# A fused convolution and channel-mix kernel: K in bundles of two slots, R's low channels as side-by-side tiles, and R and conv in two shared banks

## The chip, the cores and the metric

The kernel runs on one core of one Trainium2 chip. The metric is the device time of one execution in microseconds (us). Each kernel ran several times in rounds together with the kernel before on the same chip. Names in the trace: PE is TensorE, PEld its weight loads, DVE is VectorE, ACT is ScalarE, POOL is GpSimd, SP is SyncE.

## The reference, cut to what matters

```python
# x: (8, 4160, 192), weight: (8 heads, 7 taps)
w   = softmax(weight)
out = causal convolution of x over 7 positions, head h using w[h]     # "conv", gives y
x, x_prev = out, out shifted by one position
xk = mu_k * x + (1 - mu_k) * x_prev          # "mix"
xr = mu_r * x + (1 - mu_r) * x_prev
k  = maximum(xk @ w_k, 0)                    # 192 -> 1024      "K", "relu"
v  = k * k @ w_v                             # 1024 -> 192      "square", "V"
r  = sigmoid(xr @ w_r)                       # 192 -> 192       "R"
return r * v                                 # float32
```

The 192 channels are 128 "high" ones and 64 "low" ones. The kernel handles the batches in four pairs; for a pair, the low channels of the two batches fill partitions 0 to 63 and 64 to 127.

## The kernel before

The convolution is a product with a banded matrix, block by block of 112 positions (a "group" is several blocks). Its result y has positions on partitions. It is needed with channels on partitions, and gets there in one of two ways: by transposes on TensorE, for early groups, or by a write to DRAM and a transposing DMA read.

```python
two = ctx.enter_context(tc.tile_pool(name="two", bufs=2))
...
psK = ctx.enter_context(tc.tile_pool(name="psK", bufs=2, space=bass.MemoryType.PSUM))
psV = ctx.enter_context(tc.tile_pool(name="psV", bufs=2, space=bass.MemoryType.PSUM))
psM = ctx.enter_context(tc.tile_pool(name="psM", bufs=2, space=bass.MemoryType.PSUM))   # R, conv, transposes
...
def y_write(g):      # y -> DRAM
...
def y_read(g):       # DRAM -> yT, transposing
    nc.sync.dma_start_transpose(
        out=yTs[p][:, :, YC + r0 : YC + r1], in_=y_drams[p][r0:r1, :]
    )
...
def diff(s): ...     # d = yT[t] - yT[t-1]
def mix(s, i, part): # xk (i=0) or xr (i=1), high or low: d * mu + yT[t-1]
...
def r_mm(m):         # R of one row tile of 128
    ...
    nc.tensor.matmul(out=o, lhsT=hi, rhs=wr[:, 0, :], start=True, stop=False)
    nc.tensor.matmul(out=o, lhsT=lo, rhs=wlo, start=False, stop=True)   # 128 rows, half of wlo is zero
```

K's low channels already went as pairs of 64-row tiles that run side by side; R's did not. All work is placed by hand in tables of slots.

## Time and profile before

| kernel before | value | read from |
|---|---|---|
| time | 467.41 us (467.33 to 469.0) | 3 runs |
| span of the profiled run | 467.2 us | cores |
| TensorE, VectorE, ScalarE busy | 445.2, 390.4, 374.6 us | page, part 1 |
| TensorE's share of the chain that ended last | 91% | page, part 4 |
| clock granted to TensorE, mean | 0.990 | cores |

The prediction below shows these parts of the page and the timeline of a bundle. One more view: the waits, where each row reads "engine line waited for: us in total, times, longest us". These rows are what TensorE's convs (once the conv weights were there) and VectorE's difference waited for.

```profile
PE ps_c L199 <- DVE yT L268: 1.4, 4, 0.6
PE ps_c L199 <- ACT y L222: 0.9, 1, 0.9
DVE d L281 <- DMA yT<-y_dram: 0.2, 1, 0.2
```

### The profile page before, as it was taken

Reading aid. Unit: us, or ns where it says so; the run is one execution under the profiler, and the core shown is the slowest. Engines: PE = TensorE matmul, PEld = TensorE weight load, DVE = VectorE, ACT = ScalarE, POOL = GpSimd, SP = SyncE. Lnnn points to the kernel's source line nnn. Section 1 sums busy time; section 2 is a strip of 40 time slices with the busy share of each in tenths; the row PEclk is TensorE's granted clock in tenths of the full one; section 3 lists DMA queues with packets and bytes.
Section 4 is the critical chain, followed back from the end, with each engine's and each line's share of the span. In section 5 each row is a group of like instructions: output and inputs, shape, how many; then the busy total and the mean of one; then the engine's idle time right before and its main releaser. Section 6 shows DMA issues by size and latency. Waiting matters only on the chain.

```text
span 467.2 us, 9868 instructions
## 1 busy us (share of the span) xinstructions
PE 445.2 (95%) x3892; PEld 300.6 (64%) x3954; DVE 390.4 (84%) x616; ACT 374.6 (80%) x549; POOL 51.1 (11%) x71
## 2 busy tenths in 40 slices
PE   7788999999999999999999999999999999999996
PEld 3454766666776666666676666666676666666676
DVE  2778988797998879889798989978898987999873
ACT  2489888988879797888879788888978888777771
POOL 5812211000010041000002041000002000000000
PEclk9799999999999999999999999999999999999999
DMA  7996699972459599945367679937157753511222
GB/s 89 160 174 106 162 197 156 233 200 68 127 142 183 148 139 229 181 129 139 93 173 119 165 133 214 229 100 187 52 152 138 173 135 100 153 65 56 69 69 94
DMA packets 138942, 65.79 MB, mean 141 GB/s; under 512 B 89936, under 2 KB 138464, under 8 KB 138896
## 3 DMA queue, kind: packets, MB, share of 16 engines
q1 hardware_dynamic: 98000, 49.26, 41.0%
q0 software_dynamic: 40896, 15.90, 30.0%
q8 instruction: 31, 0.51, 0.4%
q14 instruction: 15, 0.12, 0.1%
HBM read 31.59 MB, written 37.52 MB: 148 GB/s over the span
## 4 chain that ended last, share of the span: by engine, by line
PE 91%; ACT 2%; issue 2%; DMA 2%; DVE 1%; DVEq 0%; ACTq 0%
PE ps_k L343 38%; PE ps_v L433 37%; PE ps_c L199 5%; PE ps_r L416 5%; PE ps_r L415 5%; ACT k_sb L372 1%; DMA w_scr<-w_row 1%; PE ps_k L360 1%; DMA toe<-w_scr 1%; ACT y L219 1%; DMA w_raw<-in_weight_dram 1%; PE ps_t L257 1%; DVE yT L268 0%; ACT y L222 0%; DVE k L391 0%
## 5 line engine op out<-in xcount | busy, mean ns | idle before, releaser
L372 ACT ACTIVATE k_sb<-ps_k 128x1024 bf16<-128x1024 f32 x260 | 260.2, 1026 | 35.8 <-PE ps_k L343 31.8
L343 PE MATMUL ps_k<-xk,wk 64*128 64x512 bf16 (+2 forms) x994 | 206.0, 376 | 9.5 <-ACT k_sb L372 0.9
L433 PE MATMUL ps_v<-wv,k 128*128 128x192 bf16 x2048 | 210.8, 246 | 0.0
L433 PEld LDWEIGHTS <-k 128*128 128x128 bf16 x2048 | 175.4, 98 | 30.6 <-issue 1.4
L391 DVE TENSOR_TENSOR k<-k_sb 128x1024 bf16<-128x1024 bf16 x256 | 174.8, 684 | 16.7 <-ACT k_sb L372 16.0
L343 PEld LDWEIGHTS <-wk 64*128 64x128 bf16 (+1 forms) x1056 | 56.2, 96 | 109.2 <-issue 107.9
L446 DVE TENSOR_TENSOR o_sb<-ps_v,r_sb 128x384 f32<-128x384 f32 x132 | 72.2, 547 | 39.6 <-PE ps_v L433 34.7
L423 ACT ACTIVATE r_sb<-ps_r 128x384 bf16<-128x384 f32 x132 | 64.3, 487 | 38.1 <-PE ps_r L416 37.3
L301 DVE SCALAR_TENSOR_TENSOR xr<-d,mu,yT 128x1024 bf16<-128x1024 bf16 (+1 forms) x66 | 65.1, 988 | 0.1
L301 DVE SCALAR_TENSOR_TENSOR xk<-d,mu,yT 128x1024 bf16<-128x1024 bf16 (+1 forms) x66 | 64.4, 977 | 0.2
L415 PE MATMUL ps_r<-wr,xr 128*128 128x192 bf16 x256 | 62.8, 246 | 0.0
L416 PE MATMUL ps_r<-wr,xr 128*128 128x192 bf16 x256 | 62.8, 246 | 0.0
L219 ACT CAST y<-ps_c 112x480 bf16<-112x480 f32 (+4 forms) x100 | 47.9, 483 | 10.4 <-PE ps_c L199 10.2
L199 PE MATMUL ps_c<-xb,toe 128*112 128x480 bf16 (+5 forms) x152 | 46.2, 332 | 5.3 <-DMA toe<-w_scr 2.9
L109 POOL DMA_DIRECT2D xb<-in_x_dram x38 | 34.9, 928 | 26.8 <-PE ps_c L199 15.9
L281 DVE TENSOR_TENSOR d<-yT 128x1536 bf16<-128x1536 bf16 (+2 forms) x37 | 31.8, 859 | 0.4 <-DMA yT<-y_dram 0.2
L108 POOL DMA_DIRECT2D xb<-in_x_dram x8 | 4.3, 538 | 215.7 <-PE ps_k L343 206.3
L199 PEld LDWEIGHTS <-toe 128*112 128x112 bf16 x152 | 19.2, 134 | 12.1 <-DMA toe<-w_scr 3.4
L222 ACT CAST y<-ps_c 112x480 bf16<-112x480 f32 (+8 forms) x53 | 25.2, 482 | 0.2 <-DVE yT L227 0.2
L415 PEld LDWEIGHTS <-xr 128*128 128x128 bf16 x256 | 25.0, 98 | 0.0
L416 PEld LDWEIGHTS <-xr 128*128 128x128 bf16 x256 | 25.0, 98 | 0.0
L103 POOL DMA_DIRECT2D xb<-in_x_dram x8 | 4.6, 581 | 62.4 <-PE ps_r L416 61.0
(46 smaller groups left out, 67.8 us busy)
## 6 DMA issues: line engine op xcount, KB each, us to landing
out_dram<-o_sb SPq DMA_DIRECT2D x128, 192.0 KB, 2.3
y_dram<-y SPq DMA_DIRECT2D x7, 840.0 KB, 5.0
xb<-in_x_dram POOLq DMA_DIRECT2D x12, 432.0 KB, 12.0
y_dram<-y SPq DMA_DIRECT2D x6, 756.0 KB, 4.6
xb<-in_x_dram POOLq DMA_DIRECT2D x8, 480.0 KB, 13.2
xb<-in_x_dram POOLq DMA_DIRECT2D x6, 384.0 KB, 6.6
y_dram<-y SPq DMA_DIRECT2D x2, 504.0 KB, 10.7
xb<-in_x_dram POOLq DMA_DIRECT2D x4, 240.0 KB, 5.3
```

Source lines behind the costliest of these rows:

```text
L109: nc.gpsimd.dma_start(out=xb[:, lo:hi, s, :], in_=bass.AP(tensor=x.tensor, offset=x.offset + (b * S + t0 + lo * BLK) * D, ap=[[D, P], [BLK ...
L199: nc.tensor.matmul(out=ps[:BLK, :, :, i * G : (i + 1) * G], lhsT=toe[:, h, :], rhs=xbs[g][:, :nb, :, h * G : (h + 1) * G], start=True, sto ...
L219: copy(out=yh[:, :, :, c0 : c0 + n], in_=ps[:BLK, :, :, 0:n])
L301: nc.vector.scalar_tensor_tensor(out=o, in0=d[r0:r1, sl, :L], scalar=mu[r0:r1, i, part : part + 1], in1=yT[r0:r1, sl, c0 : c0 + L], op0=AL ...
L343: nc.tensor.matmul(out=ps[:, i, f * L : (f + 1) * L], lhsT=wk[r, 0 if hi else 1, fs], rhs=xk[r, i if hi else 2, :L], start=start and f == ...
L372: nc.scalar.activation(out=k_sb, in_=ps.rearrange("p a b -> p (a b)"), func=AF.Relu)
L391: nc.vector.tensor_tensor(out=o, in0=i, in1=i, op=ALU.mult)
L415: nc.tensor.matmul(out=o, lhsT=hi, rhs=wr[:, 0, :], start=True, stop=False)
L416: nc.tensor.matmul(out=o, lhsT=lo, rhs=wlo, start=False, stop=True)
L423: nc.scalar.activation(out=r_sb[:, :n, :], in_=ps[:, :n, :], func=AF.Sigmoid)
L433: nc.tensor.matmul(out=o, lhsT=k2[:, f, t * P : (t + 1) * P], rhs=wv[:, f, :], start=(f == 0), stop=(f == NF - 1),)
L446: nc.vector.tensor_tensor(out=o_sb[:, :n, :], in0=v_ps.pop(m)[:, :n, :], in1=r_sbs.pop(m)[:, :n, :], op=ALU.mult)
```

## The change

The intent is to take work off TensorE. R's low rows of a row tile of both batches run side by side as 64-row tiles, in the stretch where K's low rows stand, so that no further turn between tile heights is needed and no multiplications by zero are done. For this, two K slots become one bundle, V of a step comes directly behind that step, R's two halves need a bank each, and R and conv share one two-bank buffer. To make the schedule fit, two more groups of the first pair are transposed on TensorE, in V's buffers, the placement was rewritten, and the warm-up (matmuls on zeros before the first conv) is longer by twelve matmuls. The core of the diff:

```diff
-    WARM = 34
+    WARM = 46
...
-    psM = ctx.enter_context(tc.tile_pool(name="psM", bufs=2, space=bass.MemoryType.PSUM))
+    psM = ctx.enter_context(tc.tile_pool(name="psM", bufs=1, space=bass.MemoryType.PSUM))
...
-            ((3, 0, True), (4, 1, True), (5, 2, True), (4, 3, True), (10, 4, False), (6, 6, False), (6, 7, False))
+            ((3, 0, True), (4, 1, True), (5, 2, True), (4, 3, True), (5, 4, True), (5, 5, True), (10, 6, False), (2, 8, False))
...
+    def m_banks():
+        shared[:] = [psM.tile([P, 2, BANK], FP32, tag="m", name="ps_m"), 2]
+        return shared[0]
+    def m_bank():
+        if shared[1] != 1:
+            m_banks()
+            shared[1] = 0
+        shared[1] += 1
+        return shared[0][:, shared[1] - 1, :]
...
-        ps = (pool or psM).tile([P, nb, 2, G * len(hs)], FP32, tag=tag, name="ps_c")
+        ps = pool.tile([P, BANK], FP32, tag="v", name="ps_c") if pool else m_bank()
...
-        ps = psM.tile([P, 3, 2, BLK], BF16, tag="m", name="ps_t")
+        ps = psV.tile([P, 3, 2, BLK], BF16, tag="v", name="ps_t")
...
+    def r_part(m, hi, start):
+        if start:
+            r_ps[m] = m_banks()
+        for i in range(2):
+            r = slice(0, P) if hi else slice(i * LO, (i + 1) * LO)
+            nc.tensor.matmul(out=r_ps[m][:, i, :D], lhsT=xr[r, i if hi else 2, cs],
+                             rhs=wr[r, 0 if hi else 1, :], start=start, stop=not start)
...
+    def conv(g, c, copy):
+        conv_mm(g, c)
+        conv_out(g, c, copy)
...
+        for c in range(nc_):
+            at(side, c0 + c // per, conv, g, c, act_)      # per is 2 in the first pair, 1 after it
...
+            at(side, e, y_write, g)
+            at(side, min(e + 3, b0 - 5), y_read, g)
...  (the order within a bundle b)
+                k_part(b, 0, True, True)
+                k_part(b, 0, False, False)
+                k_part(b, 1, False, True)
+                r_part(m, False, True)
+                k_part(b, 1, True, False)
+                r_part(m, True, False)
+            ... relus, sigmoid, V, squares, mixes (mid), output, then side: conv, transposes, y
```

## The prediction

> **What bounds the kernel now.** I began with the page: busy shares, clock row, chain.
>
> ```profile
> PE 445.2 (95%) x3892; PEld 300.6 (64%) x3954; DVE 390.4 (84%) x616; ACT 374.6 (80%) x549; POOL 51.1 (11%) x71
> ...
> PEclk9799999999999999999999999999999999999999
> ...
> PE 91%; ACT 2%; issue 2%; DMA 2%; DVE 1%; DVEq 0%; ACTq 0%
> PE ps_k L343 38%; PE ps_v L433 37%; PE ps_c L199 5%; PE ps_r L416 5%; PE ps_r L415 5%; ACT k_sb L372 1%; DMA w_scr<-w_row 1%; PE ps_k L360 1%; DMA toe<-w_scr 1%; ACT y L219 1%; DMA w_raw<-in_weight_dram 1%; PE ps_t L257 1%; DVE yT L268 0%; ACT y L222 0%; DVE k L391 0%
> ```
>
> TensorE carries 91% of the chain: K and V each over a third, R 10%. VectorE (84%) and ScalarE (80%) are close behind, so a shorter TensorE chain soon meets them. Next the timeline of TensorE alone, where no conv runs:
>
> ```profile
> 266.62 0.25 PE L415 MATMUL ps_r<-wr,xr 128*128 128x192 bf16 x1
> 266.71 0.25 PE L416 MATMUL ps_r<-wr,xr 128*128 128x192 bf16 x1
> 266.79 1.67 PE L343 MATMUL ps_k<-xk,wk 128*128 128x512 bf16 x7
> 268.30 0.82 PE L433 MATMUL ps_v<-wv,k 128*128 128x192 bf16 x8
> 268.96 0.25 PE L415 MATMUL ps_r<-wr,xr 128*128 128x192 bf16 x1
> 269.04 0.25 PE L416 MATMUL ps_r<-wr,xr 128*128 128x192 bf16 x1
> 269.12 0.82 PE L433 MATMUL ps_v<-wv,k 128*128 128x192 bf16 x8
> 269.78 0.25 PE L415 MATMUL ps_r<-wr,xr 128*128 128x192 bf16 x1
> 269.86 0.25 PE L416 MATMUL ps_r<-wr,xr 128*128 128x192 bf16 x1
> 269.95 1.67 PE L343 MATMUL ps_k<-xk,wk 128*128 128x512 bf16 x8
> ```
>
> Read the starts, for the durations overlap. Two K slots take 268.30 - 266.79 = 1.51 us, sixteen V matmuls 2 x 0.66 = 1.32, four R matmuls 4 x 0.082 = 0.33: a bundle is 3.16 us (266.79 to 269.95) without a gap. (x7 is a lost record.) From about 43 us to the end I find no gap in the starts of TensorE beyond such steps, apart from lost records. Before that there are waits; those over 0.1 us between the first K at 19.26 and 42.6 us sum to about 5.6 us, on ScalarE's and VectorE's readers and mixes. So the body falls with TensorE's own work, and the start with the other engines.
>
> The two records of a low K pair start 3 ns apart (267.317 and 267.320 us). Within the 1.51 us, high to low takes 312 ns and low to high 308 to 311 (medians), where a 512-column matmul alone takes 216: each turn costs some 95 ns.
>
> **What the Trainium skill says.** "TensorE: Matmul & The Clock Gate", Part 3 (packing small matmuls), says matmuls of few rows on different row groups run concurrently; the 3 ns agree. "TensorEngine Tiling (Array Packing)", Key Properties: changing the tiling mode drains the engine; the 95 ns agree with that. The same page, Gotcha 1, says different row tiles may not be in one PSUM bank at once: that is why R's two halves now need a bank each. "TensorE: Matmul & The Clock Gate", Part 1, says idleness over a window lowers the clock; in this trace the warm-up ends at 10.33 us, the first conv matmul is at 13.19, and the clock is half from 14.58 to 21.40 us.
>
> **The change part by part.**
> 1. *R's low channels.* Before, low rows went as 128-row matmuls against zero-padded weights: four matmuls of 82 ns per pair of row tiles. Now the two low ones run side by side as 64-row tiles, in the stretch where K's low rows already stand, so no new turn. They should take one matmul's time, 82 to 90 ns (the weight loads of such a pair take 92 to 95 ns, under the 216 ns of K ahead). R is then about 88 + 165 = 253 ns in place of 330: 77 ns saved. The bundle goes from 3.16 to 3.08 us. Of 132 K bundles, four are tails without a low stretch; with three more V bundles at the end, R makes two turns of its own in seven bundles: 190 + 88 - 165 = 113 ns dearer each. Bundles 0, 1, 4 and 5 have no R. Counted from bundle 11, behind the start: 117 x 0.077 - 7 x 0.113 = 8.2 us saved.
> 2. *Same work elsewhere.* The relu, square, sigmoid, mix and output counts remain: relu 1.02 us, square 0.68, sigmoid 0.49, output product 0.55, mixes 1.28 and 0.74, difference 0.96. Back to back they overlap by about 0.09 each. ScalarE per bundle is 0.93 + 0.40 + 0.93 = 2.26 us, with a conv copy (0.56) 2.73. VectorE has 0.60 x 2 + 0.47 + at most 1.31 (two small mixes) = 2.98. Both fit in 3.08, or 3.28 with a conv chunk (202 ns), but VectorE with a tenth of a microsecond.
> 3. *V directly behind its step.* In the last bundle of a step the second relu ends at 0.96 + 1.02 + 0.40 + 0.93 = 3.31 us; after two mixes the square ends near 4.65. V begins at 1.76 us in the next bundle, 4.84 or 5.04 on this count. It just fits; at two pair ends the tail's mixes come on top (some 1 us more work) and V may wait 0.7 us each, 1.4 in all.
> 4. *R and conv in one two-bank buffer.* A conv copy ends near 4.06 us in such a bundle, R's next low start is at 3.28 + 0.98 = 4.26. No wait with one chunk per bundle; with two (the first pair) some 0.1 to 0.3 us.
> 5. *The start.* Two groups more are transposed on TensorE: ten blocks, 30 transposes of some 50 ns, 1.5 us. These now rotate with V's two buffers: the second transpose of a bundle waits for that bundle's V product, which VectorE does some 1.6 us after V; bundles 2, 8 and 10 are hit: 4.8 us. The mixes of the first two full steps, bunched one bundle ahead, also hold K at bundles 2 and 6. Walking bundles 0 to 10 with the durations above I get bundle 11 starting at about 63.8 us. By then the kernel before would have done some 4.5 us more of TensorE work (its records up to 62 us hold about 11.5 K, 7 V and 8 R bundles and 7 conv blocks more). My walk takes K's start as in the trace at full clock; a longer warm-up (12 more matmuls of 216 ns, to about 12.9 us) may win up to 1 us or nothing.
>
> Sum: 467.4 - 8.2 + 4.5 + 1.4 - 0.5 = 464.6. The gain of the body is fairly firm; the start is a walk by hand, and its order may turn out less harmful, so I take 464.
>
> **The rivals.** *A transfer becomes the bound.* The reads of y through the transposing DMA now come three bundles before the difference that needs them (two for the long group of the first pair), and behind that bundle's output DMA on SP.
>
> ```profile
> y_dram<-y SPq DMA_DIRECT2D x7, 840.0 KB, 5.0
> ...
> yT<-y_dram SPq DMA_TRANSPOSE x15, 6.0
> ...
> DMA to landing us min/median/max: 5.3/6.0/13.5
> ```
>
> Issue at 5.5 us in its bundle plus 6 is 11.5, against the need at 12.5: fine. At the 8.7 to 13.5 us which reads beside x loads took it is 2 to 6 us late, up to three times in the run; at two bundles' lead (9.3 us) it is late anyway. PE would lose 2 to 7 us: 466 to 471. For it: the slow landings coincide with x loads. Against: the wait of VectorE on this was 0.2 us before, at a two-bundle lead too. *VectorE becomes the bound*: at 2.98 of 3.08 us any lag passes to K's mixes or to V; were the period of the 24 or so later bundles without conv 0.1 longer, that gives back 2.4 us: 467. *The start costs nothing*: if other bubbles than I think fill and the clock stays up, 467.4 - 8.2 - 1.5 = 457.7, or 455 with part of the old 5.6 us of waits gone.
>
> **Range and chances.** The centre is 464; a clean start gives 456, the late reads on top of my sum 472. All my cases but the cleanest lie within 2% (458.1 to 476.8). Range 455.5 to 472.5; faster 0.22, same 0.69, slower 0.09.
>
> **What would show it.** Two 64-row R records 3 ns apart right behind K's low ones, and 3.08 us from one K start to the next without conv: step 1. If these two low matmuls run one after the other, or the turn grows, the bundle stays near 3.16 and step 1 is wrong. VectorE's idle time before its squares would shrink, and waits of K on the mixes or of the difference on yT would show rivals one and two. PE waits before the second transposes of bundles 2, 8 and 10 would show step 5; the clock row tells of the warm-up. Wrong altogether if a stall recurs in every bundle: 0.1 us in each is 13 us.

## The result, and the profile after

| | before | after |
|---|---|---|
| time, median (range) | 468.16 us (467.33 to 469.0), 4 runs | 492.28 us (490.51 to 493.71), 4 runs |
| ratio, 95% interval | 1 | 1.0513 (1.0471 to 1.0556) |
| span of the profiled run | 467.2 us | 490.4 us |
| mean granted clock | 0.990 | 0.984 |

The kernel became slower by 5%, outside the predicted range of 455.5 to 472.5 us. All outputs are right. Ratios here are the mean time of one kernel's runs over that of the other's of the same rounds, so they are not quite the ratio of the medians. Where I turn a difference of two ratios into microseconds, I multiply by 469 us, about the median of the kernel before in the batches.

First the page of the changed kernel: busy times, TensorE's busy row and its clock row in 40 slices, and the chain that ended last.

```profile
PE 448.4 (91%) x3942; PEld 297.8 (61%) x4004; DVE 394.7 (80%) x621; ACT 384.5 (78%) x545; POOL 51.0 (10%) x71
...
PE   8776788869998999999999999999899999999996
...
PEclk9989999979999999999999999999899999999999
...
PE 67%; DVE 13%; DMA 11%; ACT 5%; issue 3%; SPq 0%; DVEq 0%; ACTq 0%
PE ps_k L358 28%; PE ps_v L445 26%; DMA yT<-y_dram 7%; DVE k L403 5%; PE ps_m L415 5%; PE ps_m L218 4%; DVE xk L320 4%; DMA y_dram<-y 4%; ACT k_sb L385 3%; PE warm L555 3%; DVE o_sb L458 2%; ACT y L238 1%; PE ps_t L276 1%; DVE tail L320 1%; ACT y L241 1%
```

TensorE's share of the chain fell from 91% to 67%; the two transfers of y took 11%. The busy row is thin in its first nine slices, the first 110 us, and the clock row dips in the same place and once later. So I put a ledger of progress beside it. Two relus are counted as one bundle in either kernel, and a row has the start of relu number 2n, counted from 0. In the first pair that is the first relu of bundle n. The tail of a pair is a bundle with a single relu, so from there on the count falls a little behind: the column 33 is the second relu of bundle 33, which opens the second pair of batches. Every value is of the one profiled execution.

| us at relu 2n, n = | 0 | 9 | 16 | 33 | 66 | 99 | 129 | end |
|---|---|---|---|---|---|---|---|---|
| before | 20.9 | 52.4 | 76.0 | 133.5 | 243.9 | 355.4 | 452.0 | 467.2 |
| after | 20.1 | 61.1 | 91.3 | 157.3 | 267.6 | 381.8 | 476.4 | 490.4 |

At bundle 33 the changed kernel is 157.3 - 133.5 = 23.8 us behind. From there to column 129 (the "body", 192 relus or 96 bundles by this count) it takes 319.1 us against 318.5. All of the loss is in the first pair, and the body, where the gain should be, gains nothing.

Next a piece of TensorE's timeline where neither conv nor waits disturb it. Columns are start, us, engine, line, operation, tiles, shapes and number.

```profile
464.82 1.13 PE L358 MATMUL ps_k<-xk,wk 128*128 128x512 bf16 x5
465.79 0.25 PE L415 MATMUL ps_m<-wr,xr 64*128 64x192 bf16 x2
465.97 0.61 PE L358 MATMUL ps_k<-xk,wk 128*128 128x512 bf16 x2
466.41 0.33 PE L415 MATMUL ps_m<-wr,xr 128*128 128x192 bf16 x2
466.57 1.48 PE L445 MATMUL ps_v<-wv,k 128*128 128x192 bf16 x16
467.89 1.13 PE L358 MATMUL ps_k<-xk,wk 128*128 128x512 bf16 x6
```

This is what was intended: two 64-row R matmuls directly behind K's low ones, whose starts lie 3 ns apart (median over the run), and 467.89 - 464.82 = 3.07 us from one bundle to the next. The loss must then lie in waits. The waits after, in the same form as before:

```profile
DVE d L300 <- DMA yT<-y_dram: 10.1, 6, 4.2
PE ps_m L218 <- ACT y L238: 9.6, 8, 4.3
PE ps_k L358 <- DVE xk L320: 8.1, 12, 2.0
PE ps_m L218 <- ACT y L241: 6.1, 7, 1.6
ACT y L238 <- DMA y_dram<-y: 3.9, 1, 3.9
PE ps_t L276 <- DVE o_sb L458: 3.3, 3, 1.5
```

TensorE's conv matmul (L218) waits 9.6 + 6.1 = 15.7 us for ScalarE's copies of y, where it had waited 0.9. VectorE's difference waits 10.1 us for the transposing read, where it had waited 0.2. The conv waits are of two kinds. The first is this one, in a bundle with two conv chunks:

```profile
73.19 0.37 PE L218 MATMUL ps_m<-xb,toe 128*112 128x480 bf16 x1
...
73.59 0.56 ACT L238 CAST y<-ps_m 112x480 bf16<-112x480 f32 x1 [0.27 <-PE ps_m L218]
...
74.20 0.36 PE L218 MATMUL ps_m<-xb,toe 128*112 128x480 bf16 x1 [0.65 <-ACT y L238]
```

In the brackets is the idle time before the instruction and what ended it. The second conv matmul starts 0.05 us after the copy of the first chunk ends at 73.59 + 0.56 = 74.15, though it writes the other bank. The two banks are one tile of the program, issued in the order matmul, copy, matmul, copy; the second writer of the tile waits for the tile's reader. The second kind occurs once:

```profile
92.41 0.42 SPq L253 DMA_DIRECT2D y_dram<-y  x1
...
96.69 0.31 PE L218 MATMUL ps_m<-xb,toe 128*112 128x96 bf16 x3
...
100.80 3.38 SPq L261 DMA_TRANSPOSE yT<-y_dram  x1
100.86 0.40 ACT L238 CAST y<-ps_m 112x288 bf16<-112x288 f32 x1 [3.89 <-DMA y_dram<-y]
101.31 0.43 PE L218 MATMUL ps_m<-xb,toe 128*112 128x96 bf16 x3 [4.31 <-ACT y L238]
```

The ten-block group ends its conv and is written to DRAM at 92.41. The next group, of two blocks, wants a new y buffer a bundle later. There are two such buffers, and the one it gets is still being written out: the transfer takes 8.38 us. The copy waits 3.89 us, TensorE 4.31. And the stall has an aftermath, seen when the first stretch is cut into windows (columns: window, length, busy us and instructions of each engine, granted clock, DMA share, GB/s):

```profile
61.00:92.00 31.00, 25.96 (x232) 16.92 (x231) 22.12 (x36) 23.23 (x34) 7.17 (x10) 1.00 0.51 80
92.00:110.00 18.00, 12.63 (x97) 7.83 (x98) 9.10 (x13) 10.19 (x17) 1.98 (x2) 0.81 0.86 174
110.00:157.00 47.00, 45.41 (x430) 32.02 (x435) 41.09 (x69) 40.80 (x59) 0.00 (x0) 1.00 0.53 123
```

In the middle window the granted clock is 0.81: it is half from 99.4 to 106.2 us. TensorE stood until 101.3 of that anyway, so by my estimate this costs at most another (106.2 - 101.3) / 2 = 2.4 us. The body's one dip is of the same sort. These are lines of the chain that ended last (start, us, what):

```profile
317.96 10.34 DMA y_dram<-y
328.32 10.43 DMA yT<-y_dram
338.77 0.07 DVE d L300
```

Write and read of y follow one another and take over 10 us each, while x loads are on their way (the queue's own view has one of 17.4 us and two with a median of 19.8 us to landing there). The difference starts 4.24 us late, K 1.96 us late at 344.98, and the clock is half from 345.1 to 348.5.

**The sum for the first pair.** By the idle times before TensorE's instructions: conv behind the copy of its neighbour 15.7 - 4.3 = 11.4 us; the y buffer 4.3 + 2.4 = 6.7; transposes waiting for V's buffer 3.3; K waiting for mixes (at 27.32, 44.38 and 155.51) 0.27 + 1.70 + 1.33 = 3.3. Together 24.7, less 3.4 of idle time that the kernel before has there (the prediction's 5.6 us for much the same stretch counts from start to start), is 21.3; with the prediction's 1.5 us for the added transposes it is 22.8, against 23.8 by the ledger. That it comes so near is in part luck: left out are R's saving of a microsecond or so and a first relu 0.8 us earlier on the one side, and V's work, which is one bundle further on, and the half clock from 27.7 to 31.1 us (1.7 us) on the other. **The sum for the body.** In TensorE's waits K waits nine times in it for a mix, 4.8 us in all (0.2 to 1.96 each), and V three times, 1.9 us (1.3 of it at two pair ends for the last square); the clock costs 1.7, together 8.4. The kernel before has no such wait in its body.

### The profile page after: what moved, and what is told of

It reads as the page before. It is cut to its first block, busy times and chain, and to the rows that moved or that the text cites. A ratio compares the mean times of both kernels' runs of the same rounds, so it can differ in the third digit from the quotient of the medians. Undisturbed runs are those within 1.5% of the kernel's fastest.

```text
span 490.4 us, 9902 instructions
## 1 busy us (share of the span) xinstructions
PE 448.4 (91%) x3942; PEld 297.8 (61%) x4004; DVE 394.7 (80%) x621; ACT 384.5 (78%) x545; POOL 51.0 (10%) x71
## 3 DMA queue, kind: packets, MB, share of 16 engines
q0 software_dynamic: 40768, 15.85, 27.7%
## 4 chain that ended last, share of the span: by engine, by line
PE 67%; DVE 13%; DMA 11%; ACT 5%; issue 3%; SPq 0%; DVEq 0%; ACTq 0%
PE ps_k L358 28%; PE ps_v L445 26%; DMA yT<-y_dram 7%; DVE k L403 5%; PE ps_m L415 5%; PE ps_m L218 4%; DVE xk L320 4%; DMA y_dram<-y 4%; ACT k_sb L385 3%; PE warm L555 3%; DVE o_sb L458 2%; ACT y L238 1%; PE ps_t L276 1%; DVE tail L320 1%; ACT y L241 1%
## 5 line engine op out<-in xcount | busy, mean ns | idle before, releaser
L358 PE MATMUL ps_k<-xk,wk 64*128 64x512 bf16 (+2 forms) x994 | 213.3, 378 | 13.5 <-DVE xk L320 8.1
L445 PE MATMUL ps_v<-wv,k 128*128 128x192 bf16 x2048 | 192.0, 247 | 2.2 <-DVE k L403 1.3
L415 PE MATMUL ps_m<-wr,xr 64*128 64x192 bf16 (+1 forms) x512 | 74.4, 248 | 0.0
L238 ACT CAST y<-ps_m 112x480 bf16<-112x480 f32 (+7 forms) x95 | 47.0, 494 | 33.3 <-PE ps_m L218 22.2
L435 ACT ACTIVATE r_sb<-ps_m 128x384 bf16<-128x384 f32 x132 | 64.2, 486 | 6.8 <-PE ps_m L415 5.9
L415 PEld LDWEIGHTS <-xr 64*128 64x128 bf16 (+1 forms) x512 | 41.1, 97 | 45.0 <-issue 2.4
L320 DVE SCALAR_TENSOR_TENSOR xr<-d,mu,yT 128x512 bf16<-128x512 bf16 (+1 forms) x66 | 65.1, 988 | 0.0
L218 PE MATMUL ps_m<-xb,toe 128*112 128x480 bf16 (+5 forms) x153 | 45.3, 324 | 15.8 <-ACT y L238 9.6
L300 DVE TENSOR_TENSOR d<-yT 128x1536 bf16<-128x1536 bf16 (+2 forms) x37 | 31.8, 860 | 10.2 <-DMA yT<-y_dram 10.1
L241 ACT CAST y<-ps_m 112x480 bf16<-112x480 f32 (+8 forms) x51 | 24.1, 472 | 5.8 <-PE ps_m L218 3.1
L218 PEld LDWEIGHTS <-toe 128*112 128x112 bf16 x160 | 18.9, 131 | 14.5 <-issue 13.7
L555 PE MATMUL warm<-zeros,ones_t 128*128 128x512 bf16 x46 | 13.0, 453 | 1.4 <-DVE zeros L536 1.4
```

Of the source, the lines that this page charges most:

```text
L218: nc.tensor.matmul(out=ps[:BLK, :, :, i * G : (i + 1) * G], lhsT=toe[:, h, :], rhs=xbs[g][:, :nb, :, h * G : (h + 1) * G], start=True, sto ...
L238: copy(out=yh[:, :, :, c0 : c0 + n], in_=ps[:BLK, :, :, 0:n])
L300: nc.vector.tensor_tensor(out=d[:, :, :L], in0=yT[:, :, c0 : c0 + L], in1=yT[:, :, c0 - 1 : c0 - 1 + L], op=ALU.subtract,)
L320: nc.vector.scalar_tensor_tensor(out=o, in0=d[r0:r1, sl, :L], scalar=mu[r0:r1, i, part : part + 1], in1=yT[r0:r1, sl, c0 : c0 + L], op0=AL ...
L358: nc.tensor.matmul(out=ps[:, i, f * L : (f + 1) * L], lhsT=wk[r, 0 if hi else 1, fs], rhs=xk[r, i if hi else 2, :L], start=start and f == ...
L415: nc.tensor.matmul(out=r_ps[m][:, i, :D], lhsT=xr[r, i if hi else 2, cs], rhs=wr[r, 0 if hi else 1, :], start=start, stop=not start,)
```

## The experiments

The theory after reading: most of the loss is the order of the two conv matmuls and their copies (first pair), the y buffer and the transfers of y come next, and the pairing of R works as intended but its gain is given back through late reads. The rivals: the pairing itself costs, through a turn or the shared banks; or V, moved directly behind its step, holds everything. Seven kernels change one thing or the sum, and three build a start without the losses. Edits are against the changed kernel. Every batch has its own runs of the kernel before: medians 469.49, 469.39 and 469.12 us. The last two columns are of the one profiled execution, which can lie off the median (486.6 us for conv matmuls first, its slowest).

| run | time, median us | ratio to before (95%) | body, us | column 33 of the ledger, us |
|---|---|---|---|---|
| changed kernel | 492.28 | 1.0513 (1.0471 to 1.0556) | 319.1 | 157.3 |
| conv matmuls first | 483.9 | 1.0307 (1.0267 to 1.0347) | 318.9 | 151.8 |
| three y buffers | 490.8 | 1.0443 (1.0400 to 1.0487) | 319.6 | 156.6 |
| R's low rows whole | 497.5 | 1.0599 (1.0574 to 1.0625) | 321.9 | 159.6 |
| transposes spread | 490.58 | 1.0452 (1.0434 to 1.0469) | 319.2 | 156.7 |
| read a bundle earlier | 488.23 | 1.0392 (1.0368 to 1.0416) | 314.5 | 158.0 |
| V a bundle later | 491.21 | 1.0489 (1.0432 to 1.0545) | 317.2 | 156.2 |
| all together | 475.92 | 1.0135 (1.0110 to 1.0160) | 311.7 | 149.2 |
| a start rebuilt | 468.62 | 0.9985 (0.9970 to 0.9999) | 311.7 | 140.7 |
| that, R's low rows whole | 473.25 | 1.0094 (1.0073 to 1.0115) | 319.4 | 138.9 |
| that, transposes shifted | 466.91 | 0.9961 (0.9941 to 0.9982) | 311.7 | 140.7 |

### Both conv matmuls before both copies

```diff
-    def conv(g, c, copy):
-        conv_mm(g, c)
-        conv_out(g, c, copy)
+    def conv(g, cs, copy):
+        for c in cs:
+            conv_mm(g, c)
+        for c in cs:
+            conv_out(g, c, copy)
...
-        for c in range(nc_):
-            at(side, c0 + c // per, conv, g, c, act_)
+        for c in range(0, nc_, per):
+            at(side, c0 + c // per, conv, g, range(c, min(c + per, nc_)), act_)
```

> One edit to the changed kernel: where a bundle has two conv chunks, both matmuls are issued before the two copies. Theory A (the loss is waits of TensorE in the first batch pair; the second chunk's matmul waits for the copy of the first because both lie in one two-bank tile, 12.5 us in all by the trace): 8 to 12 us less than the changed kernel, 480 to 484 us, and the 0.8 us waits between two conv matmuls gone. Theory B (ScalarE and VectorE are the bound in the first pair and the wait would only move to the next product): at most 3 us less, 489 us or more.

```profile
PE ps_k L358 <- DVE xk L320: 11.6, 14, 2.3
PE ps_m L218 <- ACT y L241: 5.8, 2, 5.3
```

The ratio fell by 0.0206, or 9.7 us, and the intervals lie apart. The two chunks' matmuls now run back to back, and of the conv's waits for copies (now 5.8 us) only the one for the y buffer (5.3 us) and a small one remain. This is the largest single part of the loss. It gave back less than the 11.4 us of waiting since K's waits for the mixes grew from 8.1 to 11.6 us.

### Three y buffers

```diff
-            ys[g] = two.tile([P, GB, 2 * D], BF16, tag="y", name="y")
+            ys[g] = three.tile([P, GB, 2 * D], BF16, tag="y", name="y")
```

> One edit to the changed kernel: the tile y has three buffers in place of two. Theory A (the copy of the two-block conv group waits 3.9 us for the write of y from the buffer that it reuses, TensorE stands 4.5 us and then runs 6.8 us at half clock): 5 to 9 us less, 483 to 487 us, no wait of ScalarE on the y write, no half clock near 100 us. Theory B (the transposing read that follows the same write then holds VectorE instead): at most 2 us less.

The wait of the copy for the write is gone, and TensorE's conv waits for this copy fell from 9.6 to 5.8 us. The time gained by the ratio is 0.0070 x 469 = 3.3 us, by the medians 1.5, and the intervals overlap, so the gain of this edit alone is unclear. The reason is in VectorE's timeline:

```profile
110.05 0.96 DVE L300 TENSOR_TENSOR d<-yT 128x1536 bf16<-128x1536 bf16 x1 [4.93 <-DMA yT<-y_dram]
```

The transposing read of the ten-block group, issued at 101.55, now lands after it is needed: the difference waits 4.93 us, K waits and the clock is halved again (116.3 to 119.7 us). One late transfer had stood behind the other.

### R's low rows as whole 128-row matmuls

```diff
-    wr = const.tile([P, 2, D], BF16)
+    wr = const.tile([P, 4, D], BF16)          # zero-padded again, two more loads
...
-            nc.tensor.matmul(out=r_ps[m][:, i, :D], lhsT=xr[r, i if hi else 2, cs],
-                             rhs=wr[r, 0 if hi else 1, :], start=start, stop=not start)
+            for low in range(2):              # at R's second place only
+                nc.tensor.matmul(out=r_ps[m][:, i, :D], lhsT=xr[:, 2 if low else i, cs],
+                                 rhs=wr[:, 2 + i if low else 0, :], start=not low, stop=low == 1)
```

> One part of the change undone: R's low channels as two 128-row matmuls against zero-padded weights, as before, at the place of R's high ones; all else as changed. Theory A (the pairing saves 77 ns in each bundle in which TensorE is the bound): 7 to 9 us slower than the changed kernel, 499 to 501 us. Rival (the pairing saves nothing on the path, since other engines set the pace): within 2 us of 492.

Without the pairing the kernel is slower by 0.0086, or 4.0 us. So the pairing is not the cause of the loss: it gains, even here. The result lies between the two expectations. That it gained only 4 us hangs on the late reads: at the slower pace VectorE waits for them 7.0 us in all, not 10.1, K waits for mixes 5.6 us, not 8.1, and the half clock at 345 us is missing. The run below, on the start without the losses, measures the pairing clean.

### The transposes, one pair in each bundle

```diff
-                at(side, e + j // 2, tr, g, j)
+                at(side, e + (j if g > 3 else j // 2), tr, g, j)
```

> One edit to the changed kernel: from the fifth conv group on, one transpose pair per bundle in place of two. The second of a bundle waited 1.65 us twice for the V product that holds its buffer: 2.5 to 3.5 us less, about 489 us, if the waits add; within 1 us of 492 if the next wait takes them over.

The ratio fell by 0.0061 (2.9 us), near the 3.0 us of the two long waits that it aims at. But the interval just about meets that of the changed kernel and the medians differ by only 1.7 us. In the waits the transposes still stand 2.0 us behind V's buffer, against 3.3: of the two waits of 1.49 us (the expectation had put them at 1.65) one is gone and the other is 1.64. So it is a small gain, of which the waits account for 1.3 us.

### The read of y a bundle earlier

```diff
-            at(side, min(e + 3, b0 - 5), y_read, g)
+            at(side, min(e + 2, b0 - 5), y_read, g)
```

> One edit to the changed kernel: y is read back by the transposing DMA two bundles after the end of its conv in place of three. If the late reads are a cause (the trace has VectorE waiting 10.1 us for yT, TensorE standing some 5 us behind it in the later pairs and once at half clock): 3 to 6 us less, 486 to 489 us, and no wait of the difference on yT in pairs one to three. If the reads are hidden anyway, or SP now waits for the write and delays the outputs instead: within 1.5 us of 492.

```profile
DVE d L300 <- DMA yT<-y_dram: 3.1, 2, 2.3
```

VectorE's waits for the read fell from 10.1 to 3.1 us and the body from 319.1 to 314.5 us; the ratio fell by 0.0121 (5.7 us) and the intervals lie apart. The first pair did not gain (158.0 us at bundle 33). So the late reads are the larger part of what the body's gain was lost to: 4.6 us. They are not gone, as the expectation had it; two waits remain, at 227 and 337 us.

### V a bundle later

```diff
-            tiles.append((s, c, max(b0 + nb, tiles[-1][2] + 1) if tiles else b0 + nb))
+            tiles.append((s, c, max(b0 + nb + 1, tiles[-1][2] + 1) if tiles else b0 + nb + 1))
```

> One part of the change undone: V (with its R) one bundle later than the change has it, so that no V stands right behind the squares of its step. If V right behind its step is a cause of the loss: 8 us or more less, 484 us or less. If it just fits as the prediction says, but for 0.8 us at each of three pair ends: 1 to 3 us less, 489 to 491 us.

The ratio is 1.0489 against 1.0513, well inside the intervals. V's place directly behind its step is not the cause; in the changed kernel TensorE waits for the last square twice, 1.3 us in all. Here these two waits are gone, and the result agrees with the second expectation.

### All together

The edits to the conv order, the y buffers, the transposes and the read, and besides them the mixes of the tail three bundles ahead:

```diff
+        if L == TAIL:
+            at(mid, b0 - 3, diff, s)
+            for i in range(2):
+                for part in range(2):
+                    at(mid, b0 - 3, mix, s, i, part)
+            continue
```

> Five edits together: conv matmuls before the copies, three y buffers, one transpose pair per bundle from the fifth group on, y read back one bundle earlier, the tail's mixes two to three bundles earlier. Theory A (separate waits of 12, 8, 3, 3 and 3 us that add): about 463 us, between 458 and 468. Theory B (the first pair is bound by ScalarE and VectorE): 475 us or more.

It gained 0.0378, or 17.7 us; the four single gains sum to 0.0458 (9.7 + 3.3 + 2.9 + 5.7 = 21.6 us), so a little of each lay beside another. At 475.92 us the result is where theory B had put it; the next run decides whether B's reason holds. The body falls to 311.7 us. Of the 2.7 us that it is shorter than with the early read alone, 1.3 are V's waits for the last square at two pair ends, 0.4 K's behind them and 1.0 K's behind the read that was still late: they stand in that run's trace and not in this one. What is left lies in the first pair. The next lines, of TensorE and ScalarE at 46 to 48 us and of K at two places, show it:

```profile
26.77 0.39 PE L358 MATMUL ps_k<-xk,wk 128*128 128x512 bf16 x1 [2.28 <-DVE xk L320]
...
42.91 1.27 PE L358 MATMUL ps_k<-xk,wk 128*128 128x512 bf16 x6 [2.14 <-DVE xk L320]
...
46.57 0.57 PE L218 MATMUL ps_m<-xb,toe 128*112 128x240 bf16 x4
47.18 1.02 ACT L238 CAST y<-ps_m 112x480 bf16<-112x480 f32 x2 [0.78 <-PE ps_m L218]
```

The four conv matmuls of two chunks run in 0.57 us without a wait. The first copy needs only the first two of them and yet starts when all four are done (46.57 + 0.57 = 47.14): once more the two banks behave as one. And K waits 2.28 and 2.14 us for the mixes of the first full steps, which the change bunches one bundle ahead.

### A start rebuilt

On top of all together: the last two groups of the first pair are transposed on TensorE as well, so that no transfer of y stands in it; the mixes of the first full step are earlier; and in bundles 0 to 5 the mixes come before the squares.

```diff
-            ... (5, 5, True), (10, 6, False), (2, 8, False))
+            ... (5, 5, True), (10, 6, True), (2, 8, True))
...
-                at(side, e + (j if g > 3 else j // 2), tr, g, j)
+                at(side, e + (g == 7) + (j if g > 3 else j // 2), tr, g, j)
...
-        late = 1 if b0 < 10 else 0
+        late = 1 if 2 < b0 < 10 else 0
-        at(mid, max(0, b0 - 1), mix, s, 0, 1)
+        at(mid, max(0, b0 - 1) if s > 1 else 0, mix, s, 0, 1)
...
+            if b < 6:
+                run(mid, b)
             if slots:
                 k_square(b, 0)
-            run(mid, b)
+            if b >= 6:
+                run(mid, b)
```

> The five edits of e_all, and in the first pair: the last two conv groups transposed on TensorE (no write and read of y in that pair), and the mixes ahead of the squares in the first six bundles. Theory (what e_all still loses lies in the first pair: a read of y that VectorE waited for, TensorE standing 3.9 us and half clock behind it, and K waiting 2.5 and 2.3 us for mixes): 6 to 10 us less than e_all, 465 to 470 us, level with the kernel before. If the first pair is bound by ScalarE's and VectorE's work itself: 473 us or more.

Bundle 33 starts at 140.7 us in place of 149.2, and the kernel is level with the kernel before (0.9985). After 18 us the clock is never halved, and the difference does not wait for a read at all. K's waits for the mixes fall from 7.7 to 1.7 us. So most of the rest of the loss was in the placement of the first pair, and theory B, that ScalarE's and VectorE's work itself binds there (473 us or more), is refuted. Which of these edits gained how much was not separated. It still reaches bundle 33 later than the kernel before by 7.2 us, of which part is the 66 transposes that TensorE now does for four groups (22 blocks of three), and part V's work being one bundle further.

### Two variants of the rebuilt start

The last batch, of five rounds, shifts the transposes of one more group by a bundle, once with the pairing and once without it (the edit of R's low rows is as above), so that these two differ by the pairing alone:

```diff
-                at(side, e + (g == 7) + (j if g > 3 else j // 2), tr, g, j)
+                at(side, e + (g in (5, 7)) + (j if g > 3 else j // 2), tr, g, j)
```

> e7_start with the transposes of the sixth group one bundle later, so that no bundle after the third has two. A wait of 1.65 us of TensorE goes: 1 to 2 us less than e7_start, 466.5 to 468 us, so 0.3 to 0.6% faster than the kernel before. If the wait moves on to the conv or the mixes: as e7_start, 468.6 us.

> e7_start with R's low channels as two 128-row matmuls again: what the pairing is worth once the other waits are mended. If the prediction's step 1 holds (77 ns in each bundle whose pace TensorE sets, less 7 bundles in which it costs 0.11 us): 7 to 9 us slower than e7_start, 476 to 478 us. In the changed kernel itself the same undoing cost only 4 us, as later reads then found more time. If the pairing's worth is small in itself, 4 us or less here too.

With the pairing 466.91 us, without it 473.25: a ratio lower by 0.0133, or 6.2 us: between the two expectations, nearer the 7 to 9 us of the first. The timeline of TensorE without it:

```profile
421.10 1.67 PE L360 MATMUL ps_k<-xk,wk 128*128 128x512 bf16 x7
422.61 0.49 PE L418 MATMUL ps_m<-wr,xr 128*128 128x192 bf16 x4
422.94 1.48 PE L448 MATMUL ps_v<-wv,k 128*128 128x192 bf16 x16
424.26 1.67 PE L360 MATMUL ps_k<-xk,wk 128*128 128x512 bf16 x8
```

A bundle is 424.26 - 421.10 = 3.16 us, R's four matmuls 0.33 of it, as in the kernel before. The body is 319.4 us against 311.7: 7.7 us in 96 bundles, 80 ns each. At column 33 the version with the pairing is 140.7 - 138.9 = 1.8 us later. But 1.2 us of that is there at the first relu already (20.64 against 19.40 us): its profile is of the slowest of its six runs, 468.09 us, in which the clock is half from 18.2 to 21.6 us, and the other's has no such stretch. Some 0.6 us may be the pairing's price in the first pair. R's low part, which comes first, now waits there for the conv copies that hold the two banks:

```profile
PE ps_m L415 <- ACT y L241: 1.2, 4, 0.6
```

The version with the pairing is at 0.9961 (0.9941 to 0.9982) of the kernel before, 0.4% faster. Not all of that is the change's doing in the body. Of the eleven runs of the kernel before in this batch, three had a mean clock of 0.998 and took 467.4 to 467.6 us, and eight had 0.990 to 0.993 and took 468.8 to 469.95; its profiled run (468.94 us, 0.990), of the second kind, has the clock at half from 14.6 to 21.4 us. Of the six runs of the version with the pairing, five had 0.998 or more. Set against those three, these five are faster by 0.7 us only, 0.15%. The longer warm-up may be why that stretch is rarer here; no run changed it alone.

## Why the prediction was wrong

It said 464.0 us, and 0.09 for slower by over 2%. The mechanism of the gain was right. What was wrong is the cost of the new waits.

1. **R's low channels: right.** The bundle was predicted at 3.08 us and is 3.07; the low pair starts 3 ns apart. 77 ns a bundle were predicted, 80 measured between two kernels that differ in this alone. The whole is 6.2 us against 8.2 predicted; some of the difference is the first pair, where R's low part waits for the shared banks.
2. **Same work elsewhere: right.** With the losses taken away the body takes 311.7 us, and in the last version K waits for a mix three times in it, 0.9 us in all, so VectorE as the bound did not come true.
3. **V directly behind its step: right.** 0.7 us at two pair ends was predicted, 1.4 in all; it is 1.3, and moving V back changed nothing that the runs can tell.
4. **R and conv in one two-bank buffer: this is the step that failed.** "No wait with one chunk per bundle; with two (the first pair) some 0.1 to 0.3 us." I counted when R's next start meets the copy, and treated the two chunks as two banks. They are one tile, and the diff issues matmul, copy, matmul, copy. The second matmul waited a whole copy: 11.4 us by the waits, 9.7 us by the run that only swaps the order. The sum had nothing for it.
5. **The start: its terms were near, its sum was not.** The waits before the transposes were put at 4.8 us and are 3.3. The bunched mixes of the first two full steps, which I had named without a figure, are 0.27 + 1.70 = 2.0. The longer warm-up ended at 14.3 us, not 12.9, and the first relu came 0.8 us earlier, within what I had given it. But my walk had bundle 11 starting at about 63.8 us, and it starts near 70.0 (its first relu at 70.92 less the 0.96 from K's start to it). The difference is mostly step 4's waits. The walk ended at bundle 11 and missed what came at 92 us: two y buffers with a write of 8.38 us, and the clock behind the stall, 6.7 us of loss as it stands. Removing this alone gained little, as the read then came late.
6. **Rival one came true, as an addition to the rest.** The reads were put at 2 to 6 us late where they land beside x loads, and TensorE's loss at 2 to 7 us. The difference waited 10.1 us in six places, and reading a bundle earlier gave 5.7 us back. I had held against it the 0.2 us of the kernel before. That was weak evidence: by the placement in the diff, most reads had ten slots, that is five bundles, before the difference that needs them (from n0 - 17 to n0 - 7), and the change leaves them three (from b0 - 6 to b0 - 3). This is where most of the body's gain went. The pairing gains 7.7 us in it, and the changed kernel gave back 319.06 - 311.75 = 7.3: 4.6 by the reads as far as that run mends them, 1.0 by a read that it leaves late, and 1.7 at two pair ends, which step 3 had foreseen.

In terms of the prediction's sum: 467.4 - 8.2 + 4.5 + 1.4 - 0.5 lacked about 10 us for the copies in step 4, 6 us for the reads, and some 3 to 7 us for the y buffer with its clock, 19 to 23 of the 28 us by which it missed. The rebuilt start shows a further 7 us (the ratios 1.0135 and 0.9985) in the placement of the first pair, not broken up. The prediction would have called itself wrong "if a stall recurs in every bundle"; the stalls that came were fewer and longer: some fifteen at conv chunks of the first pair, and six at reads.

What stays open: the gain of the third y buffer alone lies within the intervals, and that of the spread transposes at their very edge, measured in another batch. The longer warm-up was never changed alone. That the tile as a whole is what orders the two banks is inferred from the starts and from the gain of the swapped order; no run gave each chunk a tile of its own. No run put R's two halves into one bank either, so that they need two rests on the page that the prediction names.

## What to carry to other kernels

When two users are put into one multi-bank tile, go through the order in which its writers and readers are issued: write, read, write, read on one tile was a chain here, although each touched another bank. A walk by hand has to go on until the last buffer with a long transfer behind it has come round once, since a saving in the steady part is worth only as much as the transfers that were just in time before. A stall of TensorE should be charged with the half clock that can follow it, for the part of it in which TensorE has work again.

## What the Trainium skill lacked or had wrong

- "TensorEngine Tiling (Array Packing)", Key Properties, says that changing the tiling mode drains the engine, and gives no figure. In the kernel before a turn costs 95 ns (312 ns from start to start where 216 is the pace), and the two low R matmuls that join a stretch of their own height save 80 ns a bundle.
- "TensorE: Matmul & The Clock Gate", Part 1, has the clock fall after one or more idle windows of about 3.4 us. The half-clock stretches inside the span are indeed 3.4 or 6.8 us long, but the one at 345.1 us followed a wait of only 1.96 us, less than a window. (About 2.0 us of the 3.4 us before 345.1 were idle.)
- "Advanced Engine Details and Errata", X-Bar Transpose (TRN2), says that transposing DMAs are as fast as regular ones. The trace agrees as far as it goes (write 10.34 us, transposing read 10.43 us, one behind the other), but no page has what each takes beside other loads: the median landing of the read before was 6.0 us, and 8.5 to 10.4 us where x loads ran.
- No page says that the waits between writers and readers of a program's tile of two banks may be placed for the tile as a whole. Here the second conv matmul waited 0.65 us for the copy of the other bank of the same tile.
